# Attention with relative bias and an MLP on one core: where three pairs are turned, when one pair divides, and who copies out the last tiles

## The chip, the core and the metric

The kernel runs on one core of a Trainium2 chip. The metric is the time of one execution on the device in microseconds, as the median of several runs. A core has five engines that run their own instruction streams in order and wait for each other through semaphores: TensorE (PE, with weight loads shown apart as PEld), VectorE (DVE), ScalarE (ACT), GpSimd (POOL) and SyncE (SP). DMA transfers are issued from the streams of SP, POOL and ACT.

## The reference

Eight batches of eight heads, 576 positions, head size 64, float32. The bias depends only on the distance |i - j| through 32 buckets. Behind the attention comes an MLP with a leaky activation over 4608 tokens.

```python
scores = scale * np.matmul(q, k.transpose(0, 1, 3, 2))      # (8, 8, 576, 576)
bias = bias_table[bucket]                                     # bucket from |i - j|
scores = scores + bias.transpose(2, 0, 1)[None, :, :, :]
attn = np.exp(scores - np.max(scores, axis=-1, keepdims=True))
attn = attn / (np.sum(attn, axis=-1, keepdims=True) + 1e-09)
attn_out = np.matmul(attn, v)
x = attn_out.transpose(0, 2, 1, 3).reshape(B * S, H * D)      # (4608, 512)
h = x @ w_in                                                  # (4608, 2048)
g = np.maximum(0.01 * h, h)
out = g @ w_out                                               # (4608, 512) float32
```

## The kernel before

**Items.** The attention is worked off in 32 items, one for each batch and pair of heads, numbered from 0: item n is batch n // 4, heads 2(n % 4) and 2(n % 4) + 1. The "7th to 9th pair" of the change are items 6, 7 and 8; the 9th is the first of batch 2. For each item both heads' q and k must stand as (64 + 64) partitions by 576 positions (`qt`, `kt`); they arrive from memory as 96 rows by (head, 6 positions, 64), cast to bf16, in `qn` and `kn`.

**How q and k are turned.** There are two ways. For items 0 to 8, `turned_pair` (L267) makes twelve PE transposes for q and as many for k: each takes 96 rows of one head at one of six positions and writes 64 partitions of a PSUM bank from the pool `m`; DVE (q of early items: ACT) copies the bank to `qt` (L290) or `kt` (L294). From item 9 on (`by_dma`, L260), `pair_rows` (L252) first lays the two heads side by side in `pr` (two DVE copies of 96x768, L257), SP issues a transposing DMA from `pr` to `tu` (L265), and the same copies read `tu`.

**One body.** The loop over n (L867) runs item n's scores beside the second half of item n - 1. The order of the instructions on every engine is that of the program text. In a body: scores in PE (`qk_mm`, L312, L305 for the last 64 queries, L315 and L316 for the last 64 keys), exponentials on ACT (L325, L328, L332), the bias as a product with a band of exponentials on DVE (`band`, L348), the products with v (L361, L372 or, in halves of the rows, L407), the division on DVE (`divide`: a reciprocal L381 and a product L383 for each head, which empty the banks `o0` and `o1`), and the transposed result for the MLP (`x_transposes`: by DMA L423, or on PE L433 and a copy L434). The products L305 use `o0` and `o1` again, so they come behind the divisions. Between these stand pieces of the MLP: `ffn_in` (four products, L459, then the leaky step on ACT, L472, or on DVE, L467 and L470) and `ffn_out` (sixteen products in four parts, L486, then a copy to `y`, L504, and a store, L505). L459 and L486 take their banks from the pool `m` of two, like the transposes.

Bodies n = 5 and 6 have MLP input pieces alone (`room["only"]`): their last two pieces stand behind `band(n, 2)`, and L467 is the first DVE instruction of one of them. From n = 8 on most bodies run as `body_in_halves` (L629): there `av_phase` (L407) and pieces of the MLP (L610) run on the two halves of PE's rows, `fence` (L391) orders them, `transpose_q(n + 1)` stands ahead of `band(n, 0)` and `divide(n - 1, range(2))`, which divides both heads at once, and `score(n, 4)` (L305) follows behind the last L610 products. Body n = 8 is the first that copies q (of item 9) from a DMA's rows; that DMA is issued in body n = 7.

**Loads.** POOL issues all loads of q, k, v and the weights (L112 to L241), early items far ahead of their use; q and k of batch 2, first half of the heads, are issued in body n = 2.

**The end.** After the last item, `moe_rest` (L726) runs the rest of the MLP; its banks rotate over six. The last 128 products on PE are eight groups of sixteen L486: four of token tile 7, four of token tile 8. Seven groups are copied by DVE and stored by SP; the last group is copied and stored as two halves of 256 columns, one by DVE and SP, one by ACT and ACT's own queue (L491 to L498). Both halves read one PSUM bank, and the second copy waits for the first.

Of the kernel before, what the change touches and what calls it, by code (L numbers as in the profile page):

```python
# [37 lines left out]
def kernel(  # L38
# [10 lines left out]
    nc = tc.nc  # L49
# [217 lines left out]
    def turned_pair(n, j):  # L267

        if by_dma(n):
            return turned[n][:, j * NC : (j + 1) * NC, :].rearrange("p c r -> p r c")  # L270
        ps = ps_m_pool.tile([P, 8 * P], BF16, name="ps_t", tag="m")
        b, p = items[n]
        for c in range(NC):
            for e in range(2):
                nc.tensor.transpose(ps[e * D : (e + 1) * D, c * RQ : (c + 1) * RQ],
                                    in_=(qn, kn)[j][b % NBUF][0:RQ, 2 * p + e, c, :],
                                    identity=ident[0:RQ, 0:RQ])
        return ps[:, 0:S].rearrange("p (c r) -> p r c", c=NC)
# [55 lines left out]
    def band(n, u):  # L334
        b, p = items[n]
        at, at4 = at_view(n), at4_[n % 2]
        hp = hk[:, 2 * p : 2 * p + 2, :]
        if u == 0:
            o, m = at[:, :, 0, 0 : 2 * P], mirrored(hp, P, 3 * P)
        elif u in (1, 2):  # L340
            o, m = at[:, :, u, (u - 1) * P : (u + 2) * P], mirrored(hp, 0, 3 * P)
        elif u == NJ:
            o, m = at[:, :, 3, 2 * P : S], mirrored(hp, 0, S - 2 * P)
        elif u == NJ + 1:
            o, m = at4[:, 3 * P : S], mirrored(hk4[:, p, :], 0, P + SL)
        else:
            return
        nc.vector.tensor_tensor(out=o, in0=o, in1=m, op=ALU.mult)  # L348
# [27 lines left out]
    def divide(n, heads):  # L376
        opair = ops_[n]
        of = [outs[n][e][:, 0 : (NJ + 1) * (D + 1)].rearrange("p (i d) -> p i d", d=D + 1) for e in heads]
        rcps = [rc_pool.tile([P, NJ + 1, 1], FP32, name="rcp") for _ in heads]
        for ps, rcp in zip(of, rcps):  # L380
            nc.vector.reciprocal(rcp, ps[:, :, D : D + 1])  # L381
        for e, ps, rcp in zip(heads, of, rcps):
            nc.vector.tensor_tensor(out=opair[:, :, e * D : (e + 1) * D], in0=ps[:, :, 0:D],  # L383
                                    in1=rcp.to_broadcast([P, NJ + 1, D]), op=ALU.mult)
# [4 lines left out]
    def fence(sooner):  # L389

        f = nc.sync.nop(nofuse=True)  # L391
        tc.add_manual_dep(f.ins, sooner.ins.name, ended, reason="behind the last products of these rows")
        return f
# [83 lines left out]
    def ffn_out(T, s):  # L477

        t0 = T * TT
        gt, ts, part = gts[T], s // 4, s % 4  # L480
        if part == 0:
            outs_pm[T] = bank("pm2")
        pm = outs_pm[T]
        n = n_fc // 4
        for f in range(part * n, (part + 1) * n):
            nc.tensor.matmul(pm, lhsT=gt[:, f, ts * P : (ts + 1) * P], rhs=w_out_sb[:, f, :],  # L486
                             start=(f == 0), stop=(f == n_fc - 1))
        if part < 3:
            return
        o = out[t0 + ts * P : t0 + (ts + 1) * P, :]  # L490
        if T == n_tt - 1 and s == n_fc - 1:  # L491
            h = DM // 2
            for copy, queue, d in ((nc.vector.tensor_copy, nc.sync, slice(0, h)),
                                   (nc.scalar.copy, nc.scalar, slice(h, DM))):
                y = y_pool.tile([P, DM], FP32, name="y")
                copy(out=y[:, 0:h], in_=pm[:, d])
                queue.dma_start(out=o[:, d], in_=y[:, 0:h])
            return  # L498
        y = y_pool.tile([P, DM], FP32, name="y")
        if how["scalar"]:  # L500
            nc.scalar.copy(out=y, in_=pm)
            stores.append((o, y))
            return
        nc.vector.tensor_copy(out=y, in_=pm)  # L504
        nc.sync.dma_start(out=o, in_=y)  # L505
# [123 lines left out]
    def body_in_halves(n, kinds):  # L629

        loads(n)
        turns = rows_ahead(n) if by_dma(n + 1) else []
        score(n, 0)
        av_tails(n - 1)
        last = fence(av_phase(n - 1, 0))
        score(n, 1)
        T, s = made["out"], at_piece["out"]
        if kinds[0] == "out":
            one, two = open_piece("out", (T, s)), open_piece("out", (T, s + 4))
        else:  # L640
            one, two = open_piece("in"), open_piece("out")
        phase = side_by_side(one, two)
        phase(0, 0, 1)
        av_phase(n - 1, 1, last)
        if n + 1 < N:
            transpose_q(n + 1)
        band(n, 0)
        divide(n - 1, range(2))
        last = fence(phase(0, 1, n_cc))
        score(n, 2)  # L650
        score(n, 3)
        phase(1, 0, n_cc, last)
        band(n, 1)
        if n + 1 < N:
            transpose_k(n + 1)
        score(n, 4)
        if kinds[0] == "in":
            one[2]()
        late = [n - 1]
        if x_by_dma(n - 1):  # L660
            x_transposes(late.pop())
        for m in turns:
            turn_by_dma(m)
        while stores:
            o, y = stores.pop(0)
            nc.sync.dma_start(out=o, in_=y)
        band(n, 2)
        if kinds[0] == "out":
            outs_pm[T] = one[0]
            ffn_out(T, s + 1)  # L670
            band(n, 4)
            score(n, 5)
            band(n, 5)
            ffn_out(T, s + 2)
            ffn_out(T, s + 3)
            for m in late:
                x_transposes(m, "o0")
                finished(m)
            outs_pm[T] = two[0]
            for part in range(5, 8):  # L680
                ffn_out(T, s + part)
            at_piece["out"] = (s + 8) % n_fc
            made["out"] += at_piece["out"] == 0
            return
        piece_out()
        band(n, 4)
        score(n, 5)
        band(n, 5)
        piece_out()
        piece_out()  # L690
        for m in late:
            x_transposes(m, "o1")
            finished(m)
        room["left"] -= 5
        moe(room["left"], 0)
# [166 lines left out]
    moe(2)  # L862
    band(n, 5)
    band(n, 4)
    moe(1)

    for n in range(n_pairs + 1, N + 1):  # L867
# [43 lines left out]
            band(n, 1)  # L911
        band(n, 2)
        if room["only"]:
            exp(n, 3, ps_b)
            moe(2)
            exp(n, 4, ps_c)
            score(n, 5)
            T, f = step("in")
            room["left"] -= 1

            def last_bands():
                band(n, 5)
                band(n, 4)

            leaky(T, f, ffn_in(T, f), True, last_bands)
            moe(room["left"])
            continue
# [44 lines left out]
```

## Time and profile before

| | |
|---|---|
| Median of 3 runs | 375.03 us (374.81 to 375.28) |
| The profiled execution, its own time | 375.26 us |
| Its span, first to last instruction | 373.5 us |
| Granted clock of TensorE | 1.000 |
| Busy: PE, ACT, DVE, POOL | 357.6, 240.7, 196.5, 76.8 us |
| Items 9 on: DMA from `pr` to `tu` | 23 issues, 5.1 us from issue to landing (median) |
| Stores of 256 KB | 35, 2.4 us from issue to landing (median) |

How to read it: the chain of waits is followed back from the last instruction, at each step to what released it. A timeline row has the start in us, the length in us, the engine, the line, the operation and what it writes and reads; in brackets stands the idle time of the engine before it and what ended it. A row of the chain has start, length, engine, tile and line. In rows by group the length is the mean of one instruction in ns. PE's products overlap one another, so one lasts longer (379 ns for 512 columns) than the distance from one to the next.

### The profile page before, as it was taken

Reading aid. Unit: us, or ns where it says so; the run is one execution under the profiler, and the core shown is the slowest. Engines: PE = TensorE matmul, PEld = TensorE weight load, DVE = VectorE, ACT = ScalarE, POOL = GpSimd, SP = SyncE. Lnnn points to the kernel's source line nnn. Section 1 sums busy time; section 2 is a strip of 40 time slices with the busy share of each in tenths; the row PEclk is TensorE's granted clock in tenths of the full one; section 3 lists DMA queues with packets and bytes.
Section 4 is the critical chain, followed back from the end, with each engine's and each line's share of the span. In section 5 each row is a group of like instructions: output and inputs, shape, how many; then the busy total and the mean of one; then the engine's idle time right before and its main releaser. Section 6 shows DMA issues by size and latency. Waiting matters only on the chain.

```text
span 373.5 us, 10548 instructions
## 1 busy us (share of the span) xinstructions
PE 357.6 (96%) x4473; PEld 187.1 (50%) x4516; DVE 196.5 (53%) x504; ACT 240.7 (64%) x374; POOL 76.8 (21%) x118
## 2 busy tenths in 40 slices
PE   7889999999999999999999999999999999999994
PEld 2455555555455555555555555555555544444441
DVE  4688577776758566666755656665554200100121
ACT  5898886568856787777877777777777264064000
POOL 8763431333023303330233023100000000000000
PEclk9999999999999999999999999999999999999999
DMA  8999999999669979977798589833121000200221
GB/s 106 177 198 181 207 203 143 150 165 163 78 86 173 124 127 125 152 112 150 97 121 130 98 112 133 119 80 79 43 32 40 30 28 0 86 28 0 86 84 59
DMA packets 104360, 40.19 MB, mean 108 GB/s; under 512 B 83184, under 2 KB 98808, under 8 KB 104312
## 3 DMA queue, kind: packets, MB, share of 16 engines
q0 software_dynamic: 53696, 18.36, 47.6%
q1 hardware_dynamic: 50472, 21.02, 28.1%
q8 instruction: 35, 0.57, 0.6%
q10 hardware_dynamic: 144, 0.13, 0.1%
q14 instruction: 13, 0.11, 0.1%
HBM read 37.68 MB, written 9.45 MB: 126 GB/s over the span
## 4 chain that ended last, share of the span: by engine, by line
PE 87%; DVE 5%; ACT 4%; DMA 2%; issue 2%; DVEq 0%; ACTq 0%
PE pm L459 28%; PE pm L486 27%; PE pm L610 8%; PE ps_s L312 7%; PE ps_o L407 6%; PE ps_o L372 4%; ACT at L325 2%; DMA tu<-pr 2%; PE ps_s L315 2%; PE ps_o L361 1%; DVE opair L383 1%; PE ps_w L747 1%; DVE at L348 1%; PE ps_tx L433 1%; PE ps_q L305 1%
## 5 line engine op out<-in xcount | busy, mean ns | idle before, releaser
L325 ACT ACTIVATE at<-ps_s 128x1024 bf16<-128x1024 f32 x128 | 124.6, 1028 | 24.9 <-PE ps_s L312 24.8
L472 ACT ACTIVATE gt<-pm 128x512 bf16<-128x512 f32 x138 | 82.9, 605 | 71.1 <-PE pm L459 70.5
L459 PE MATMUL pm<-xT,w_in_sb 128*128 128x512 bf16 x490 | 117.2, 379 | 1.1
L486 PE MATMUL pm<-w_out_sb,gt 128*128 128x512 bf16 x468 | 109.3, 379 | 3.3 <-issue 3.0
L348 DVE TENSOR_TENSOR at<-at,hk 128x768 bf16<-128x768 bf16 (+3 forms) x160 | 71.0, 454 | 58.6 <-ACT at L325 34.2
L459 PEld LDWEIGHTS <-w_in_sb 128*128 128x128 bf16 x508 | 47.7, 98 | 54.7 <-issue 0.7
L486 PEld LDWEIGHTS <-gt 128*128 128x128 bf16 x492 | 45.0, 98 | 51.4
L504 DVE COPY y<-pm 128x512 f32<-128x512 f32 x35 | 24.2, 691 | 74.8 <-PE pm L486 72.1
L312 PE MATMUL ps_s<-qt,kt 64*128 64x512 bf16 x256 | 43.2, 380 | 3.6 <-ACT at L325 3.0
L610 PE MATMUL pm<-w_out_sb,gt 64*128 64x512 bf16 x168 | 42.0, 376 | 0.0
L610 PE MATMUL pm<-xT,w_in_sb 64*128 64x512 bf16 x136 | 37.5, 376 | 0.0
L119 POOL DMA_DIRECT2D vn<-in_v_dram x32 | 29.8, 939 | 11.1 <-PE pm L459 4.2
L383 DVE TENSOR_TENSOR opair<-ps_o,rcp 128x320 bf16<-128x320 f32 x64 | 29.7, 488 | 1.6
L769 POOL COPY tick<-opair 1x1 bf16<-1x1 bf16 x18 | 3.5, 194 | 130.5 <-DVE opair L383 130.5
L407 PE MATMUL ps_o<-vn,at 64*128 64x65 bf16 x1520 | 29.5, 190 | 0.0
L407 PEld LDWEIGHTS <-at 64*128 64x128 bf16 x1520 | 27.1, 94 | 4.3 <-SPq L391 3.0
L312 PEld LDWEIGHTS <-kt 64*128 64x128 bf16 x256 | 11.6, 94 | 25.5 <-issue 16.5
L332 ACT ACTIVATE at<-ps_s 128x576 bf16<-128x576 f32 x32 | 21.8, 683 | 0.7 <-PE ps_s L316 0.7
L381 DVE RECIPROCAL rcp<-ps_o 128x5 f32<-128x5 f32 x64 | 10.0, 181 | 22.3 <-PE ps_o L372 19.3
L328 ACT ACTIVATE at<-ps_q 128x256 bf16<-128x256 f32 x64 | 21.4, 396 | 0.5 <-PE ps_q L305 0.4
L372 PE MATMUL ps_o<-vn,at 128*128 128x65 bf16 x520 | 20.1, 194 | 0.0
L372 PEld LDWEIGHTS <-at 128*128 128x128 bf16 x520 | 17.9, 98 | 3.5 <-issue 0.7
(62 smaller groups left out, 243.3 us busy)
## 6 DMA issues: line engine op xcount, KB each, us to landing
out_dram<-y SPq DMA_DIRECT2D x35, 256.0 KB, 2.4
qn<-in_q_dram POOLq DMA_DIRECT2D x14, 288.0 KB, 6.3
kn<-in_k_dram POOLq DMA_DIRECT2D x14, 288.0 KB, 7.1
vn<-in_v_dram POOLq DMA_DIRECT2D x28, 128.0 KB, 5.9
w_in_sb<-in_moe_w_in_dram POOLq DMA_DIRECT2D x2, 1024.0 KB, 12.3
w_out_sb<-in_moe_w_out_dram POOLq DMA_DIRECT2D x2, 1024.0 KB, 15.8
qn<-in_q_dram POOLq DMA_DIRECT2D x4, 144.0 KB, 3.8
kn<-in_k_dram POOLq DMA_DIRECT2D x4, 144.0 KB, 4.0
```

What stands on the lines that cost most here:

```text
L119: nc.gpsimd.dma_start(out=vn[b % NBUF][:, c, h0:h1, 0:D], in_=v[b, h0:h1, c * P : (c + 1) * P, :].rearrange("h s d -> s h d"),)
L312: nc.tensor.matmul(ps[:, e, :], lhsT=kt[r, u * P : (u + 1) * P], rhs=qt[r, 0:512], start=True, stop=True)
L325: nc.scalar.activation(at[:, :, u, 0:512], ps, AF.Exp, scale=scale)
L348: nc.vector.tensor_tensor(out=o, in0=o, in1=m, op=ALU.mult)
L372: nc.tensor.matmul(ps[:, ic, :], lhsT=at[:, o : o + P], rhs=vn[b % NBUF][:, c, 2 * p + e, :], start=False, stop=(ic == NJ and c == NJ - 1))
L383: nc.vector.tensor_tensor(out=opair[:, :, e * D : (e + 1) * D], in0=ps[:, :, 0:D], in1=rcp.to_broadcast([P, NJ + 1, D]), op=ALU.mult)
L407: m = nc.tensor.matmul(outs[n][e][:, ic * (D + 1) : (ic + 1) * (D + 1)], lhsT=at[halves[r], o : o + P], rhs=vn[b % NBUF][halves[r], c, 2 * ...
L459: nc.tensor.matmul(pm, lhsT=w_in_sb[:, c, f * P : (f + 1) * P], rhs=xT[c][:, t0 : t0 + TT], start=(c == 0), stop=(c == n_cc - 1))
L472: nc.scalar.activation(g, pm, AF.Prelu, bias=0.0, scale=1.0, alpha=0.01)
L486: nc.tensor.matmul(pm, lhsT=gt[:, f, ts * P : (ts + 1) * P], rhs=w_out_sb[:, f, :], start=(f == 0), stop=(f == n_fc - 1))
L504: nc.vector.tensor_copy(out=y, in_=pm)
L610: m = nc.tensor.matmul(pm, lhsT=w[halves[r]], rhs=x[halves[r]], start=(k == 0 and c == 0), stop=(low is not None and k == 1 and c == n_cc ...
```

## The change

It has three parts.

1. `pair_rows` is also called for items 6, 7 and 8: for item 6 at the end of body n = 4 (behind `band(4, 4)`), for items 7 and 8 in bodies n = 5 and 6 behind `band(n, 2)`, ahead of the last MLP pieces. `turned_pair` then makes six PE transposes of 96 rows by 128 columns (both heads) instead of twelve of 96 by 64. On DVE that adds three times two copies of 96x768; on PE 36 transposes with their weight loads fall away, and 36 of the double width stay where 72 stood.
2. In body n = 8, `transpose_q(9)` moves behind `band(8, 0)` and `divide(7, ...)`. On DVE the copy L290 thus follows the two L381 and two L383 instead of standing ahead of the band.
3. Once all input pieces of the MLP are made, output tiles are copied by ACT and stored from ACT's queue instead of by DVE and SP: seven tiles of 128x512. The last group's parts 0 to 2 do nothing; with part 3 it runs sixteen products of 384 columns in one bank and then sixteen of 128 columns in another, each part copied by ACT and stored from ACT's queue behind its last product.

No other instruction changes its place on any engine.

```diff
@@ turned_pair
         for c in range(NC):
+            if n > n_pairs + 1:
+                nc.tensor.transpose(ps[:, c * RQ : (c + 1) * RQ], in_=prs[n][:, j, c, :],
+                                    identity=ident[0:RQ, 0:RQ])
+                continue
             for e in range(2):
@@ ffn_out
         n = n_fc // 4
+        o = out[t0 + ts * P : t0 + (ts + 1) * P, :]
+        if T == n_tt - 1 and ts == 3:
+            if part < 3:
+                return
+            for d in (slice(0, 3 * P), slice(3 * P, DM)):
+                w = d.stop - d.start
+                pm = bank("pm2")
+                for f in range(n_fc):
+                    nc.tensor.matmul(pm[:, 0:w], lhsT=gt[:, f, ts * P : (ts + 1) * P], rhs=w_out_sb[:, f, d],
+                                     start=(f == 0), stop=(f == n_fc - 1))
+                y = y_pool.tile([P, DM], FP32, name="y")
+                nc.scalar.copy(out=y[:, 0:w], in_=pm[:, 0:w])
+                nc.scalar.dma_start(out=o[:, d], in_=y[:, 0:w])
+            return
         for f in range(part * n, (part + 1) * n):
...
-        o = out[t0 + ts * P : t0 + (ts + 1) * P, :]
-        if T == n_tt - 1 and s == n_fc - 1:
-            h = DM // 2
-            for copy, queue, d in ((nc.vector.tensor_copy, nc.sync, slice(0, h)),
-                                   (nc.scalar.copy, nc.scalar, slice(h, DM))):
-                y = y_pool.tile([P, DM], FP32, name="y")
-                copy(out=y[:, 0:h], in_=pm[:, d])
-                queue.dma_start(out=o[:, d], in_=y[:, 0:h])
-            return
         y = y_pool.tile([P, DM], FP32, name="y")
         if how["scalar"]:
             nc.scalar.copy(out=y, in_=pm)
             stores.append((o, y))
+            return
+        if made["in"] == n_tt:
+            nc.scalar.copy(out=y, in_=pm)
+            nc.scalar.dma_start(out=o, in_=y)
             return
         nc.vector.tensor_copy(out=y, in_=pm)
         nc.sync.dma_start(out=o, in_=y)
@@ body_in_halves
         av_phase(n - 1, 1, last)
-        if n + 1 < N:
+        late_q = n == 2 * n_pairs
+        if n + 1 < N and not late_q:
             transpose_q(n + 1)
         band(n, 0)
         divide(n - 1, range(2))
+        if late_q:
+            transpose_q(n + 1)
         last = fence(phase(0, 1, n_cc))
@@ body n = n_pairs
     band(n, 5)
     band(n, 4)
+    pair_rows(n + 2)
     moe(1)
@@ loop over n
         band(n, 2)
         if room["only"]:
+            if not by_dma(n + 2):
+                pair_rows(n + 2)
             exp(n, 3, ps_b)
             moe(2)
```

## The prediction, made before the changed kernel ran

> **What bounds it now.** I read the page first, then the chain of waits merged in order of time, then the timeline of the places where that chain leaves TensorE.
>
> ```profile
> span 373.5 us, 10548 instructions
> PE 357.6 (96%) x4473; PEld 187.1 (50%) x4516; DVE 196.5 (53%) x504; ACT 240.7 (64%) x374; POOL 76.8 (21%) x118
> PE 87%; DVE 5%; ACT 4%; DMA 2%; issue 2%; DVEq 0%; ACTq 0%
> ```
>
> TensorE (PE) carries 87% of the chain. So work taken from PE, or a gap of PE closed, shortens the run; work added to VectorE (DVE) or ScalarE (ACT) costs only where PE ends up waiting for it. The one large piece of the chain off PE is a DMA, around the body n = 8 (items count from 0: the 7th to 9th pairs are items 6 to 8):
>
> ```profile
> 59.68 7.71 DMA tu<-pr
> 67.42 0.65 DVE qt L290
> ...
> 69.99 0.81 PE pm L486 x3
> ```
>
> It does not hold PE for 7.7 us; the timeline of that place shows what it does cost:
>
> ```profile
> 66.44 0.78 PE L407 MATMUL ps_o<-vn,at 64*128 64x65 bf16 x40
> 66.54 0.35 DVE L257 COPY pr<-kn 96x768 bf16<-96x768 bf16 x1
> 67.42 0.65 DVE L290 COPY qt<-tu 128x576 bf16<-128x576 bf16 x1 [0.53 <-DMA tu<-pr]
> 67.99 0.42 DVE L348 TENSOR_TENSOR at<-at,hk 128x512 bf16<-128x512 bf16 x1
> 68.13 1.03 PE L610 MATMUL pm<-w_out_sb,gt 64*128 64x512 bf16 x8
> 68.32 0.26 DVE L381 RECIPROCAL rcp<-ps_o 128x5 f32<-128x5 f32 x2
> 68.61 0.89 DVE L383 TENSOR_TENSOR opair<-ps_o,rcp 128x320 bf16<-128x320 f32 x2
> 69.56 0.27 PE L305 MATMUL ps_q<-qt,kt 64*128 64x64 bf16 x7 [0.19 <-DVE opair L383]
> ```
>
> DVE stands 0.53 us until item 9's transposed rows land, then copies q (0.65); only then do the band and the two divisions (L381, L383) follow. PE's products of L305 write the banks that the divisions read, so PE waits for L383.
>
> **Part 1, the divisions ahead of q's copy (n = 8).** The next body shows the same place without the wait:
>
> ```profile
> 78.69 0.38 PE L610 MATMUL pm<-xT,w_in_sb 64*128 64x512 bf16 x1
> 79.55 0.28 PE L305 MATMUL ps_q<-qt,kt 64*128 64x64 bf16 x8
> 79.99 0.38 PE L486 MATMUL pm<-w_out_sb,gt 128*128 128x512 bf16 x1 [0.16 <-issue]
> 69.89 0.65 DVE L294 COPY kt<-tu 128x576 bf16<-128x576 bf16 x1
> 75.57 0.39 PE L312 MATMUL ps_s<-qt,kt 64*128 64x512 bf16 x2
> ```
>
> The first three rows are n = 9. From the start of its eight L610 products (the first row is one of them) it is 0.86 to L305 and 1.30 to L486. For n = 8 that would be 68.13 + 0.86 = 68.99 and 68.13 + 1.30 = 69.43; L486 started at 69.99 (the chain above): the stall is 0.56 us. In the changed order DVE is free at 66.54 + 0.35 = 66.89, does the band (0.42) to 67.3, starts the reciprocals when L407 has ended (66.44 + 0.78 = 67.22), and has divided by 67.3 + 0.26 + 0.89 = about 68.55, 0.4 ahead of 68.99. The stall goes whole: -0.56. What moves behind is q's copy, to 68.55 to 69.2: it no longer waits (the rows landed at 67.40), k's copy of item 9 (69.89, fourth row) stays within 0.1 us, and the scores that use both start at 75.57. Its cover is those 6 us; without it, it would cost its 0.65. Bounds: 0 and -0.56.
>
> **Part 2, whole pairs transposed on PE.** Six sets (q and k of items 6, 7, 8) of twelve 96x64 transposes become six of 96x128. Rows for the size:
>
> ```profile
> 48.56 0.38 PE ps_t L275 x12
> 56.54 0.72 PE ps_o L372 x20
> 72.77 0.28 PE ps_tx L433 x5
> L372 PEld LDWEIGHTS <-at 128*128 128x128 bf16 x520 | 17.9, 98 | 3.5 <-issue 0.7
> ```
>
> A set takes 0.38 now. A 128x128 transpose costs 0.28/5 = 56 ns. The 512-column products pass a column in 0.42 ns (Part 3), so 128 columns are 54 of the 56, and 96 columns are 40; with 3 over, 43 ns, so 0.26 a set: -0.12. Ends: 63 ns (a pair of halves as now, 0.38/6; no gain) and 40 ns (-0.14). For q the whole 0.12 reaches the path in all three bodies, as PE goes straight on to L459, the second head and its reciprocal: -0.36 (0 to -0.42). For k in n = 5 and 6 something else ends last:
>
> ```profile
> 42.09 0.49 DVE L383 TENSOR_TENSOR opair<-ps_o,rcp 128x320 bf16<-128x320 f32 x1
> 42.50 0.75 DVE L294 COPY kt<-ps_t 128x576 bf16<-128x576 bf16 x1
> 43.30 1.89 PE L459 MATMUL pm<-xT,w_in_sb 128*128 128x512 bf16 x7
> ```
>
> L459 needs the bank that k's copy empties at 43.25, and that copy starts behind a division, not behind the transposes; 0 there (to -0.28). In n = 7 PE has no such wait: -0.12 (0 to -0.14).
>
> DVE pays with three times two copies of 96x768, about 0.35 each (the L257 row above), in gaps it has:
>
> ```profile
> 39.90 0.20 DVE L381 RECIPROCAL rcp<-ps_o 128x5 f32<-128x5 f32 x1 [2.83 <-PE ps_o L372]
> 46.33 0.69 DVE L467 TENSOR_SCALAR low<-pm 128x512 bf16<-128x512 f32 x1 [1.52 <-PE pm L459]
> 55.02 0.69 DVE L467 TENSOR_SCALAR low<-pm 128x512 bf16<-128x512 f32 x1 [1.53 <-PE pm L459]
> 35.20 0.67 POOL L112 DMA_DIRECT2D kn<-in_k_dram  x1 [0.24 <-DMA vn<-in_v_dram]
> kn<-in_k_dram POOLq DMA_DIRECT2D x1, 288.0 KB, 14.8
> ```
>
> The copies stand just ahead of these three instructions, 0.70 into gaps of 2.83, 1.52 and 1.53: nothing, and 0.70 each if the gap were gone, because L467, the last bands and L470 queue behind them. Item 8's rows are the latest to arrive, at 35.20 + 14.8 = 50.0, against a read at 55.02 - 1.53 = 53.5.
>
> **Part 3, the last rows.** Now:
>
> ```profile
> 340.60 27.51 PEld L486 LDWEIGHTS <-gt 128*128 128x128 bf16 x128
> 368.64 0.42 DVE L496 COPY y<-pm 128x256 f32<-128x256 f32 x1 [2.76 <-PE pm L486]
> 369.10 0.37 ACT L496 COPY y<-pm 128x256 f32<-128x256 f32 x1 [27.49 <-DVE y L496]
> 369.50 0.37 ACTq L497 DMA_DIRECT2D out_dram<-y  x1
> L472 ACT ACTIVATE gt<-pm 128x512 bf16<-128x512 f32 x138 | 82.9, 605 | 71.1 <-PE pm L459 70.5
> out_dram<-y SPq DMA_DIRECT2D x7, 256.0 KB, 2.0
> out_dram<-y SPq DMA_DIRECT2D x1, 128.0 KB, 1.7
> out_dram<-y ACTq DMA_DIRECT2D x1, 128.0 KB, 2.5
> q14 instruction: 3, 0.02, 1.5%
> ```
>
> The two half copies run one behind the other: DVE's starts 0.02 after PE's end (368.62), ACT's ends at 369.47: 0.85. Afterwards the last group is 16 products of 384 columns, then 16 of 128. The 128 weight loads start 27.4/127 = 216 ns apart, one 512-column product each, so 384 take 162 and 128 take 56 (the L433 row): 3.49 against 3.45, +0.04. The 384 part is copied and issued while PE makes the 128 part (0.9 us): the copy takes about 0.49 and the issue 0.37, just in time. ACT from 256 to 512 columns goes from 372 to 605 ns, 0.91 a column, so the 128-column copy takes 256: 0.28 after PE's end, -0.57. Seven full copies also go from DVE to ACT (about 0.6 every 3.45 us; ACT did nothing there) and their stores from SP's queue to ACT's: nothing, as PE alone sets that stretch, and a full copy and issue would have to outlast 3.45 us to cost. Landing: the last store now takes 2.5, though SP's equal half took 1.7 and a store of twice the size 2.0; in that stretch instruction fetches (q14) run on the same engines. I take 2.0 for the 64 KB, between 1.7 and 2.5, since the fetch may meet it again: -0.5 (0 to -0.8).
>
> The Trainium skill, page "DMA: Bandwidth & Descriptors", section "Anatomy of one DMA", fits 2.0 us + bytes/436e9 for GpSimd's path; by it (an estimate) 64 KB land in 2.15, 0.35 sooner than now instead of 0.5; SP's 1.7 lies under its fixed part.
>
> **Sum**: -0.56 - 0.36 - 0.12 + 0.04 - 0.57 - 0.5 = -2.07. Against the profiled execution's own 375.26: 373.2. That execution lies 0.23 above the median of the runs, so the median goes from 375.03 to **373.0**.
>
> **Rivals.**
> - The 64-wide halves already pass side by side, and a whole one takes as long as two. For: twelve in 0.38 are 32 ns each, less than the 40 that 96 columns need. Against: the L433 row. Part 2 brings 0: 373.5.
> - PE's gain in the middle (1.04) is given back at a later wait: some operand that comes by DMA is met 1 us sooner. For: DMA is busy there. Against: item 9's is the only such wait in the list. Only the tail stays, -1.03: 374.0.
> - As before, and the last store again lands in 2.5: -0.53, 374.5, not told from no change (0.2%, 0.75 us, is about what can be).
> - Slower: a stationary operand of 128 columns whose load is not hidden. 36 transposes and 16 narrow products would each cost its 98 ns (L372 row): 36 x 0.098 - 6 x 0.38 = +1.25, tail 16 x (0.098 + 0.162) - 3.45 = +0.71, less 0.56 and 0.57, landing 2.5: +0.83, 375.9. It decides from 82 ns a product on. Against: L372's twenty with 128x128 weights take 0.72, 36 ns each.
>
> The Trainium skill, page "TensorE: Matmul & The Clock Gate", section "Part 3: Packing small matmuls", says that a weight load overlaps running products only where its row group differs; all these use the same rows, so it speaks for that last rival. The trace disagrees: 36 ns a pair against loads of 98.
>
> **How the numbers follow.** Forecast 0.50; halves side by side 0.18; only the tail 0.17; as before 0.10; slower 0.05. Faster by over 0.2% (under 374.28): 0.50 + 0.18 + 0.17 = 0.85; within 0.10; slower 0.05. The largest gain of all bounds is 0.56 + 0.42 + 0.28 + 0.14 + 0.53 + 0.8 = 2.73, 372.3; the upper end takes in the tail-only case: 372.2 to 374.3.
>
> **What would show it.** Right: a set of six transposes in about 0.26; no idle time of DVE at q's copy of item 9 and L486 1.3 behind the eight L610's start; from the last product to the last issue about 0.3; the last store landing near 2.0. Wrong: a set still at 0.38; L305 still waiting for L383; an idle PE behind L467 or the pair copies; a landing of 2.5; a gap that opens behind n = 9.

## The result and the profile after

| | before | after |
|---|---|---|
| Median | 375.03 us (374.81 to 375.28) | 372.27 us (372.04 to 372.53, 4 runs) |
| Ratio, with its 95% interval | | 0.9921 (0.9908 to 0.9933) |
| The profiled execution, its own time | 375.26 us | 372.35 us |
| Its span | 373.5 us | 370.6 us |

The kernel became faster by 2.8 us in the medians, 2.9 in the two profiled executions. The forecast was 373.0, 0.7 above the measured median; the median stands at the low end of the range (372.2), and the ratio times 375.03, 372.07, lies 0.1 below it. The longest runs had a lower granted clock: the five longest of the kernel before among the experiments (377.1 us and over) had a mean clock of 0.991 to 0.996, and the longest run without part 1 there, 379.64 us at 0.991, is left out of its ratio.

Lines of the changed kernel are shifted: L376 is L372 of before, L463 is L459, L504 is L486, L623 is L610, L387 is L383, L316 is L312, L309 is L305, L471 is L467, and q's copy L294 is L290. L275 is now the whole-pair transpose and L279 the one in halves.

The page of the changed kernel, the busy times and the chain by engine:

```profile
span 370.6 us, 10507 instructions
PE 356.3 (96%) x4453; PEld 187.7 (51%) x4496; DVE 192.9 (52%) x502; ACT 245.4 (66%) x382; POOL 76.4 (21%) x118
PE 87%; ACT 4%; DMA 3%; DVE 3%; issue 2%; POOL 0%; ACTq 0%; DVEq 0%; POOLq 0%
```

PE's busy time fell by 1.3 us only, and its share of the chain is still 87%: the rest of the 2.9 us are idle stretches, so they have to be looked for place by place.

**The transposed sets.** PE's timeline of before, first the surroundings of q's set in n = 5, then the first of the four score products at four points (start, length, engine, line, what it writes and reads, count):

```profile
38.39 0.61 PE L312 MATMUL ps_s<-qt,kt 64*128 64x512 bf16 x4
...
39.08 0.78 PE L372 MATMUL ps_o<-vn,at 128*128 128x65 bf16 x20
39.79 0.45 PE L275 MATMUL ps_t<-ident,qn 96*64 96x96 bf16 x12
40.17 1.04 PE L459 MATMUL pm<-xT,w_in_sb 128*128 128x512 bf16 x3
...
47.09 0.61 PE L312 MATMUL ps_s<-qt,kt 64*128 64x512 bf16 x4
...
55.78 0.61 PE L312 MATMUL ps_s<-qt,kt 64*128 64x512 bf16 x4
...
60.48 0.61 PE L312 MATMUL ps_s<-qt,kt 64*128 64x512 bf16 x4
```

The same view of the changed kernel:

```profile
38.14 0.60 PE L316 MATMUL ps_s<-qt,kt 64*128 64x512 bf16 x4
...
38.83 0.78 PE L376 MATMUL ps_o<-vn,at 128*128 128x65 bf16 x20
39.45 0.42 PE L275 MATMUL ps_t<-ident,pr 96*128 96x96 bf16 x6
39.71 1.03 PE L463 MATMUL pm<-xT,w_in_sb 128*128 128x512 bf16 x3
...
46.61 0.61 PE L316 MATMUL ps_s<-qt,kt 64*128 64x512 bf16 x4
...
55.08 0.61 PE L316 MATMUL ps_s<-qt,kt 64*128 64x512 bf16 x4
...
59.33 0.61 PE L316 MATMUL ps_s<-qt,kt 64*128 64x512 bf16 x4
```

From score to score it was 8.70, 8.69 and 4.70 us; it is 8.47, 8.47 and 4.25. That is -0.23 for n = 5, -0.22 for n = 6 and -0.45 for n = 7 (the last stretch holds both of its sets): -0.90, where the prediction had -0.48. The six whole transposes pass in 39.71 - 39.45 = 0.26 instead of 0.38, as forecast. But by the starts the row ahead of them became shorter too: the set now begins 0.62 behind the start of the twenty products, 0.71 before. That second piece, 0.09 a set, was not in the sum. The chain of waits, which goes by ends, has it on the row behind the set instead; this is that row in the chain of before and in that of the changed kernel, n = 5:

```profile
40.24 0.32 PE pm L459
```

```profile
39.87 0.22 PE pm L463
```

The first row also shows something that the change does not touch: the changed kernel was already 0.25 ahead at 38 us, where both programs had run the same transposes. That is scatter from execution to execution: in two further executions of the changed kernel (below) the same point lies at 38.82 and 38.58.

**DVE's cover.** DVE's timeline, the instruction behind the two pair copies in n = 5 and in n = 6:

```profile
45.86 0.69 DVE L471 TENSOR_SCALAR low<-pm 128x512 bf16<-128x512 f32 x1 [0.98 <-PE pm L463]
...
54.32 0.69 DVE L471 TENSOR_SCALAR low<-pm 128x512 bf16<-128x512 f32 x1 [0.99 <-PE pm L463]
```

DVE still waits 0.98 and 0.99 us for PE there (1.52 and 1.53 before), so the copies, which take 0.54 of each gap, delay nobody.

**Body n = 8.** The changed kernel's timeline, DVE and PE:

```profile
66.45 0.89 DVE L387 TENSOR_TENSOR opair<-ps_o,rcp 128x320 bf16<-128x320 f32 x2
66.99 1.03 PE L623 MATMUL pm<-w_out_sb,gt 64*128 64x512 bf16 x8
67.85 0.28 PE L309 MATMUL ps_q<-qt,kt 64*128 64x64 bf16 x8
68.18 0.76 DVE L294 COPY qt<-tu 128x576 bf16<-128x576 bf16 x1 [0.84 <-DMA tu<-pr]
68.29 0.81 PE L504 MATMUL pm<-w_out_sb,gt 128*128 128x512 bf16 x3 [0.16 <-issue]
```

L623 to L309 is 0.86 and to L504 1.30, the distances of a body without the stall. DVE waited for item 9's rows even longer than before (0.84, not 0.53), but now the divisions stand ahead of that wait, and PE lost nothing. The lead over before grew from 1.15 us at the last score row above to 69.99 - 68.29 = 1.70 at L504: 0.55, forecast 0.56.

**Body n = 25.** The chain, and PE's timeline at its end:

```profile
214.65 9.21 DMA xT<-opair
```

```profile
223.13 0.37 PE L623 MATMUL pm<-xT,w_in_sb 64*128 64x512 bf16 x1
...
223.90 0.37 PE L623 MATMUL pm<-xT,w_in_sb 64*128 64x512 bf16 x1 [0.39 <-DMA xT<-opair]
```

Two products that otherwise start 0.22 apart started 0.77 apart, since the transposed rows of item 23 landed 9.2 us after their issue. 0.55 us of the lead went here, in this one execution: in the two further profiled executions of the same kernel (below) PE does not wait at this place.

**The end.** The timeline of PE and ACT, and the last two stores (queue, operation, count, size, us to landing):

```profile
363.85 3.66 PE L497 MATMUL pm<-w_out_sb,gt 128*128 128x384 bf16 x32
...
367.60 0.27 ACT L500 COPY y<-pm 128x128 f32<-128x128 f32 x1 [0.47 <-PE pm L497]
367.89 0.34 ACTq L501 DMA_DIRECT2D out_dram<-y  x1
```

```profile
out_dram<-y ACTq DMA_DIRECT2D x1, 192.0 KB, 1.9
out_dram<-y ACTq DMA_DIRECT2D x1, 64.0 KB, 1.6
```

PE ends at 363.85 + 3.66 = 367.51. The last copy ends at 367.87, 0.36 later (0.85 before); the store is issued at 367.89 and lands in 1.6 (2.5 before), at 369.49; the span ends 1.1 later (373.5 - 369.50 - 2.5 = 1.5 before). From PE's end to the end of the span it is 3.09 us, 4.88 before: -1.79, forecast -1.07.

The whole account of the profiled pair: start -0.25, sets -0.90, n = 8 -0.55, n = 25 +0.55, narrow products and rounding +0.04, end -1.79: -2.90. The first and the fourth are not the change's own.

### The profile page after: what moved, and what is told of

Read it like the earlier page. It is cut to its first block, busy times and chain, and to the rows that moved or that the text cites. A ratio compares the mean times of both kernels' runs of the same rounds, so it can differ in the third digit from the quotient of the medians.

```text
span 370.6 us, 10507 instructions
## 1 busy us (share of the span) xinstructions
PE 356.3 (96%) x4453; PEld 187.7 (51%) x4496; DVE 192.9 (52%) x502; ACT 245.4 (66%) x382; POOL 76.4 (21%) x118
## 4 chain that ended last, share of the span: by engine, by line
PE 87%; ACT 4%; DMA 3%; DVE 3%; issue 2%; POOL 0%; ACTq 0%; DVEq 0%; POOLq 0%
PE pm L463 28%; PE pm L504 27%; PE pm L623 8%; PE ps_s L316 8%; PE ps_o L411 6%; PE ps_o L376 4%; DMA xT<-opair 2%; ACT at L329 2%; PE ps_s L319 2%; PE ps_o L365 1%; DVE opair L387 1%; PE ps_tx L437 1%; PE ps_q L309 1%; DMA kn<-in_k_dram 1%; PE pm L497 1%
## 5 line engine op out<-in xcount | busy, mean ns | idle before, releaser
L463 PE MATMUL pm<-xT,w_in_sb 128*128 128x512 bf16 x490 | 117.2, 379 | 1.1
L504 PE MATMUL pm<-w_out_sb,gt 128*128 128x512 bf16 x452 | 105.9, 379 | 3.3 <-issue 3.0
L463 PEld LDWEIGHTS <-w_in_sb 128*128 128x128 bf16 x508 | 47.8, 98 | 54.5 <-issue 0.7
L504 PEld LDWEIGHTS <-gt 128*128 128x128 bf16 x476 | 43.5, 98 | 49.5
L316 PE MATMUL ps_s<-qt,kt 64*128 64x512 bf16 x256 | 43.3, 380 | 3.6 <-ACT at L329 3.0
L623 PE MATMUL pm<-w_out_sb,gt 64*128 64x512 bf16 x168 | 42.2, 376 | 0.0
L517 DVE COPY y<-pm 128x512 f32<-128x512 f32 x28 | 19.4, 691 | 40.9 <-PE pm L504 38.1
L623 PE MATMUL pm<-xT,w_in_sb 64*128 64x512 bf16 x136 | 37.7, 376 | 0.4 <-DMA xT<-opair 0.4
L387 DVE TENSOR_TENSOR opair<-ps_o,rcp 128x320 bf16<-128x320 f32 x64 | 29.7, 488 | 1.6
L316 PEld LDWEIGHTS <-kt 64*128 64x128 bf16 x256 | 11.6, 94 | 25.4 <-issue 16.5
L376 PE MATMUL ps_o<-vn,at 128*128 128x65 bf16 x520 | 20.1, 194 | 0.0
L376 PEld LDWEIGHTS <-at 128*128 128x128 bf16 x520 | 17.9, 98 | 3.5 <-issue 0.7
```

Source lines behind the costliest of these rows:

```text
L316: nc.tensor.matmul(ps[:, e, :], lhsT=kt[r, u * P : (u + 1) * P], rhs=qt[r, 0:512], start=True, stop=True)
L376: nc.tensor.matmul(ps[:, ic, :], lhsT=at[:, o : o + P], rhs=vn[b % NBUF][:, c, 2 * p + e, :], start=False, stop=(ic == NJ and c == NJ - 1))
L463: nc.tensor.matmul(pm, lhsT=w_in_sb[:, c, f * P : (f + 1) * P], rhs=xT[c][:, t0 : t0 + TT], start=(c == 0), stop=(c == n_cc - 1))
L623: m = nc.tensor.matmul(pm, lhsT=w[halves[r]], rhs=x[halves[r]], start=(k == 0 and c == 0), stop=(low is not None and k == 1 and c == n_cc ...
```

## The experiments

The kernel before, run again beside these kernels on three chips, scattered more than in the first runs: medians 375.56, 375.56 and 375.45 (57 runs, 374.55 to 378.1). Each ratio below is against the runs of before on the same chip; a kernel with one run has no interval.

| kernel | median us (lowest to highest, runs) | ratio (95%) |
|---|---|---|
| part 1 alone | 375.79 (374.54 to 377.43, 12) | 1.0008 (0.9990 to 1.0027) |
| part 2 alone | 374.34 (373.35 to 375.76, 12) | 0.9963 (0.9947 to 0.9980) |
| part 3 alone | 373.48 (373.00 to 373.99, 6) | 0.9944 (0.9926 to 0.9962) |
| the change again | 372.40 (372.21 to 372.52, 4) | 0.9913 (0.9893 to 0.9932) |
| the change a third time | 372.36 (372.21 to 374.82, 6) | 0.9921 (0.9897 to 0.9945) |
| without part 1 | 374.04 (372.84 to 379.64, 7) | 0.9952 (0.9932 to 0.9972) |
| without the seven full tiles on ACT | 373.66 (373.14 to 375.25, 11) | 0.9944 (0.9925 to 0.9963) |
| before, 8 more DVE instructions | 374.57 (374.17 to 377.36, 11) | 0.9974 (0.9954 to 0.9994) |
| items 4 and 5 whole too | 373.54 (373.02 to 374.08, 6) | 0.9942 (0.9924 to 0.9960) |
| halves out of `pr` | 373.17 (1) | |
| only the k sets whole | 373.28 (1) | |
| one position of six in halves | 374.04 (1) | |

### Each part alone, and all of them again

Each is the kernel before with one part of the diff shown above; the fourth kernel is the changed one.

```diff
@@ part 1 alone: body_in_halves
-        if n + 1 < N:
+        late_q = n == 2 * n_pairs
+        if n + 1 < N and not late_q:
             transpose_q(n + 1)
...
+        if late_q:
+            transpose_q(n + 1)
@@ part 2 alone: turned_pair, and the two calls of pair_rows
+            if n > n_pairs + 1:
...
+    pair_rows(n + 2)
...
+            if not by_dma(n + 2):
+                pair_rows(n + 2)
@@ part 3 alone: ffn_out
+        if T == n_tt - 1 and ts == 3:
...
+        if made["in"] == n_tt:
```

> Only the divisions ahead of q's copy in body n = 8; all else as before. My account: DVE's wait for item 9's rows goes and PE's wait for the divisions with it, 0.56 us between bodies 8 and 9 and nowhere else, so 374.5 if the gain lasts to the end. Rival: the gain is given back at a later DMA operand (in the changed kernel 0.57 us went again in body n = 25, where PE waited for xT); then 375.0.

> Only the transposes of whole pairs for items 6 to 8; all else as before. My account now: a set saves 0.22 us, 0.12 in the transposes themselves and 0.10 in the step from the 128x65 products to them; both sets of bodies 7 and the q sets of bodies 5 and 6 reach the path: 0.88 us by body 8, 374.15. As recorded: 0.12 a set, 0.48 in all, 374.55. Item 9's rows are then the later ones at body 8, so DVE's wait there should grow and may take back part of the 0.88.

> Only the change at the end (copies and stores by ACT, last rows in two parts); all else as before. My account: the end comes 0.56 us earlier by the copies, 0.9 by the landing, 0.4 by SP's last waits, less 0.05 to 0.1 for the narrow products: 1.8 us, 373.2. As recorded: 1.03, 374.0, with the last store landing in 2.0.

> The changed kernel once more. If the wait for xT in body n = 25 belongs to the new times, it is there again and the runs lie at 372.3. If it came from one late transfer, it is gone or elsewhere in this profile, and the span is nearer 370.0.

Against before on the same chip the parts bring +0.23, -1.22 and -2.08, together -3.07; all of them together -3.16. That the two agree is luck: each interval is 1.2 to 1.5 us wide, part 1's gain is not in its median, and part 2 alone also ends 0.7 sooner, because its last store lands in 1.8 us and not in 2.5, a gain that part 3 brings as well.

The profiles add up better. From the first scores of n = 5 to PE's end it is 330.21 us before (38.39 to 368.60), 329.64 with part 1 alone, 329.37 with part 2 alone, and 328.80 with all parts, in two executions (329.37 in the first one, with its wait in n = 25). So part 1 gives 0.57 there, part 2 0.84 and both together 1.41. From PE's end to the end of the span it is 4.9 before and with part 1 alone, and 3.1 with part 3 alone and with all of them.

Part 2 alone shows the scores at 39.42, 47.90, 56.36 and 60.61 us: stretches of 8.48, 8.46 and 4.25, a gain of 0.90 again, of which 0.05 goes to a longer stall in n = 8 (0.61, with a wait of 0.60 for item 9's rows). Part 3 alone has the same end as the changed kernel: its last store is issued at 368.54, lands in 1.6, and the span ends at 371.2, 1.1 after that. In part 1 alone PE's timeline has the eight L610 products at 68.65 and L486 at 69.95, the 1.30 of a body without the stall, and by the sums above the gain lasts to PE's end. In the time of that execution (375.27) it isn't seen, since it came to the first scores of n = 5 at 38.92, 0.53 later than before. That point lies anywhere from 38.14 to 39.46 in the fourteen profiles, also for one and the same kernel; what sets it is open. It is open too why the median of the twelve runs shows no gain: their interval (0.9990 to 1.0027) leaves out one of 0.56 us (0.9985). The counter-experiment (without part 1) is below.

In the second execution of the whole change PE doesn't wait in n = 25, nor in the third. So that wait is not a property of the change; none of the other thirteen profiles has it. The span did not come near 370.0 all the same: it was 370.7, as the first scores of n = 5 came 0.68 later than in the first execution.

### Part 2: what a set of halves costs

The recorded term was 0.12 a set, the traces show 0.22. Three kernels look for the rest: the halves taken out of `pr` (is it the source?), the k sets alone whole (which sets reach the path?), one of the six positions left in two halves (is it the halves, or the switch between them and whole products?).

```diff
@@ halves out of pr
             if n > n_pairs + 1:
-                nc.tensor.transpose(ps[:, c * RQ : (c + 1) * RQ], in_=prs[n][:, j, c, :],
-                                    identity=ident[0:RQ, 0:RQ])
+                for e in range(2):
+                    nc.tensor.transpose(ps[e * D : (e + 1) * D, c * RQ : (c + 1) * RQ],
+                                        in_=prs[n][:, j, c, e * D : (e + 1) * D],
+                                        identity=ident[0:RQ, 0:RQ])
@@ only the k sets whole
-            if n > n_pairs + 1:
+            if n > n_pairs + 1 and j == 1:
@@ one position of six in halves
-            if n > n_pairs + 1:
+            if n > n_pairs + 1 and c != NC // 2:
```

> The changed kernel, but the rows in pr are again turned in twelve 96x64 transposes a set: the source, DVE's copies and all else stay. Before, the halves started in pairs every 43 ns, the rate of the whole ones now; what a set of halves costs more would then be the two steps into it and out of it, about 0.09 us each. So: from the first L376 to the first L463 behind q's set 1.09 us again (0.88 in the changed kernel), bodies 5, 6 and 7 longer by 0.22, 0.22 and 0.44. Rival: the source made the difference (qn and kn against pr); then bodies as in the changed kernel.

> The changed kernel, but only k's sets are whole pairs; q's are twelve halves. If k's gain in bodies 5 and 6 is hidden behind DVE's copy of k, as recorded, these two bodies are as long as before the change (8.70 from scores to scores) and body 7 alone is 0.22 shorter than before. Rival: k's sets gain 0.22 in each of the three.

> The changed kernel, but of the six positions of each set the fourth is turned as two halves, the other five whole. If the two steps between whole and half operands cost 0.09 us each, a set loses nearly all its gain: bodies 5, 6 and 7 are longer by 0.2, 0.2 and 0.4 than in the changed kernel. If each half product were the dearer one, a sixth of 0.22 is lost: 0.04, 0.04 and 0.07.

Halves out of `pr`, PE's timeline, the last two score rows (L318 is L316 there):

```profile
56.02 0.61 PE L318 MATMUL ps_s<-qt,kt 64*128 64x512 bf16 x4
...
60.72 0.60 PE L318 MATMUL ps_s<-qt,kt 64*128 64x512 bf16 x4
```

4.70, the distance of before: where the rows come from makes no difference. With only the k sets whole:

```profile
47.67 0.61 PE L316 MATMUL ps_s<-qt,kt 64*128 64x512 bf16 x4
...
56.36 0.61 PE L316 MATMUL ps_s<-qt,kt 64*128 64x512 bf16 x4
...
60.83 0.60 PE L316 MATMUL ps_s<-qt,kt 64*128 64x512 bf16 x4
```

n = 5 takes 8.70 (from 38.97) and n = 6 8.69 as before, so k's set brings nothing there, and n = 7 takes 4.47 instead of 4.70, so it brings 0.23. That is the prediction's split of the sets: three for q and one for k, 4 x 0.22 = 0.88. With one position in halves, PE's timeline of q's set in n = 5:

```profile
40.15 0.78 PE L376 MATMUL ps_o<-vn,at 128*128 128x65 bf16 x20
40.77 0.29 PE L275 MATMUL ps_t<-ident,pr 96*128 96x96 bf16 x3
40.99 0.23 PE L279 MATMUL ps_t<-ident,qn 96*64 96x96 bf16 x2
41.16 0.26 PE L275 MATMUL ps_t<-ident,pr 96*128 96x96 bf16 x2
41.26 1.03 PE L463 MATMUL pm<-xT,w_in_sb 128*128 128x512 bf16 x3
```

This set holds five whole products and one pair of halves, and from L376 to L463 it takes 1.11, no less than the 1.09 of before with six pairs. At 43 ns a product the first three should last 0.13, but it is 0.22 to the halves; the pair should last 0.04, but it is 0.17 to the next whole one. The last two go at the usual pace (0.10). So the halves themselves cost no more than whole products, a pair of them in 43 ns; going from products that use the whole width of PE to such that use half, and back, costs 0.09 + 0.13 = 0.22 us, and once a set, with one pair of halves between as with six. The three bodies take 8.71, 8.69 and 4.70 in this kernel, as before the change. In the trace's single records of before, the load of the first half of this set starts 0.15 us behind the load ahead of it, and that of the first L459 0.18 behind the last half's, where loads, or pairs of them, otherwise follow each other at 0.03 to 0.04: at both switches the next load starts late. Why it does is not shown.

### The end: landing, pauses and the seven tiles

Before, the last store (128 KB) landed in 2.5 us, its equal on SP's queue in 1.7. Two suspects: the instruction fetches (q14), which share the DMA engines, and ACT's queue itself. Eight more instructions on DVE ahead of `moe_rest` move the rest of DVE's stream and leave the code of the end as it is:

```diff
@@ moe_rest of the kernel before
+        for _ in range(8):
+            nc.vector.memset(warm, 0.0)
```

> The kernel before with eight memsets of one column on DVE ahead of the last MLP part, where DVE has nothing to do. If the last store of before landed late (2.5 us) because an instruction fetch, set off by the count of DVE's instructions, met it on one DMA engine, the fetch now comes earlier: landing 1.75, the end about 0.5 to 0.7 us earlier than before with the same copies. Rival: ACT's queue is slower at its first store; then 2.5 again and no change.

The last stores of this kernel in the view of its DMA:

```profile
out_dram<-y SPq DMA_DIRECT2D x1, 128.0 KB, 1.7
out_dram<-y ACTq DMA_DIRECT2D x1, 128.0 KB, 1.7
```

The same store on the same queue lands in 1.7 now. The view of the DMA, taken over the time in which this store's packets move, has two instruction fetches in before (369.5 to 371.5 us) and in part 1 alone (369.46 to 371.51), where the landing is 2.5 as well. It has none in this kernel up to 372.6 (one begins at 372.63, beside the last packets), and none in part 2 alone (369.69 to 371.1), which has six more DVE instructions and the end of before, and lands in 1.8. So the queue is not the cause: the store lands late where two fetches fall among its packets. That they are fetches of DVE's instructions, and meet it on the same DMA engine, is inferred; no row names either. The last 1.5 us, from landing to the end of the span, stay as they were. In the medians this kernel is 0.99 us faster than before, more than the 0.7 of its end; its profiled execution, 376.32, is one of its longest, because of a long stall in n = 8 (below).

For the other two pieces of the end, the seven full tiles went back to DVE and SP, and only the last group kept its new form:

```diff
@@ ffn_out of the changed kernel
-        if made["in"] == n_tt:
-            nc.scalar.copy(out=y, in_=pm)
-            nc.scalar.dma_start(out=o, in_=y)
-            return
```

> The changed kernel, but the seven full tiles at the end are copied by DVE and stored by SP as before; only the last group is ACT's. Copies and landing as in the changed kernel (0.29 and 1.6). If SP's 0.37 us pause among its last waits belongs to SP's own instruction count, it is back with SP's seven stores and the end is 0.4 later than in the changed kernel: 372.8. Rival: the pause went with the order of the last stores; then 372.4.

Its timeline of the end:

```profile
364.23 3.66 PE L497 MATMUL pm<-w_out_sb,gt 128*128 128x384 bf16 x32
...
367.54 0.37 ACTq L501 DMA_DIRECT2D out_dram<-y  x1
368.46 0.27 ACT L500 COPY y<-pm 128x128 f32<-128x128 f32 x1 [0.95 <-PE pm L497]
368.75 0.34 ACTq L501 DMA_DIRECT2D out_dram<-y  x1
```

PE ends at 367.89, and the last copy starts at 368.46, 0.57 later instead of 0.09, although ACT had been through with the issue at 367.91. The view by line shows the semaphore waits at L500, here (from 366 us on) and in the changed kernel (from 364 us on; the first of its two stands ahead of the first copy):

```profile
L500 ACTq EVENT_SEMAPHORE  x3: 38/38/38, 368.2 to 368.4; - x3
```

```profile
L500 ACTq EVENT_SEMAPHORE  x2: 17/17/17, 365.0 to 367.5; - x2
```

So ACT has three waits ahead of this copy and not one. But the first of the three starts only 0.32 us after the issue (0.04 in the changed kernel), and they follow each other at 0.08: of the 0.48 that the copy is later, about 0.28 is this pause and 0.2 are the waits. In before, a pause of the same 0.32 stands at the same place of ACT's stream, behind its 575th record of the trace; there it falls behind the last issue and holds up no copy. The store lands in 1.6 again, at 370.35, and the span ends at 371.9: 1.55 later, 1.1 in the changed kernel. So without the seven tiles the end is longer by 0.48 + 0.45 = 0.93, of the 1.3 us that the medians differ by (on different chips; 0.9 to 1.2 by the ratios). Only the 0.4 was expected. PE itself is not touched: from the first scores of n = 5 to its end it is 328.80, as in the changed kernel.

The 1.5 us stand in all five kernels that have the seven stores on SP's queue (before, part 1 alone, part 2 alone, 8 more instructions, this one), the 1.1 in the nine that don't. The trace's records of SP's last waits show why: in each of the five a pause of 0.34 to 0.36 us stands behind SP's 207th record, after the landing of the last store (372.14 to 372.49 in before). The nine have 198 records on SP and no such pause. So it is SP's own stream that ends later, and the order of the last stores, which is the new one here, is not the reason. What the two pauses are stays open.

### Part 1 taken away

```diff
-        late_q = n == 2 * n_pairs
+        late_q = False
```

> The changed kernel with q's copy of item 9 ahead of the band and the divisions again. Bodies 5 to 7 now end 0.9 us sooner while item 9's rows land about as late as before, so DVE waits longer for them and PE for DVE: at least 0.56 us more between bodies 8 and 9, 372.9 to 373.5, and more where the transfer is late in a run. Rival: part 1 is worth nothing in the time, as the comparison of part 1 alone read (375.79 against 375.56); then 372.4.

Its timeline of n = 8:

```profile
67.06 1.03 PE L623 MATMUL pm<-w_out_sb,gt 64*128 64x512 bf16 x8
67.15 0.65 DVE L294 COPY qt<-tu 128x576 bf16<-128x576 bf16 x1 [1.34 <-DMA tu<-pr]
68.35 0.89 DVE L387 TENSOR_TENSOR opair<-ps_o,rcp 128x320 bf16<-128x320 f32 x2
68.89 0.20 PE L309 MATMUL ps_q<-qt,kt 64*128 64x64 bf16 x1 [0.81 <-DVE opair L387]
69.72 0.81 PE L504 MATMUL pm<-w_out_sb,gt 128*128 128x512 bf16 x3 [0.16 <-issue]
```

L623 to L504 takes 2.66 instead of 1.30: the stall is 1.36 here, 0.56 in the profile of before, because the rows were waited for 1.34 instead of 0.53. In the profile of the kernel with eight more DVE instructions (DVE's timeline) the wait is longer still:

```profile
69.20 0.65 DVE L290 COPY qt<-tu 128x576 bf16<-128x576 bf16 x1 [2.00 <-DMA tu<-pr]
```

There the stall is 2.03, which is why that execution was long. Part 3 alone has a wait of 0.31 and a stall of 0.33. So with the old order the stall follows the landing of item 9's rows, which differs from execution to execution, and the divisions ahead of the wait take it out whole, whatever its length (0.84 us of waiting in the changed kernel cost nothing). Beside the other two parts, part 1 is worth 374.04 - 372.36 = 1.68 in the medians, 1.2 by the ratios (0.9952 against 0.9921, of 375; the intervals overlap), and 1.36 in the profile, more than the 0.56 of the prediction each time.

### Further whole pairs, and the change a third time

If a set gives 0.22, items 4 and 5 might give it too.

```diff
@@ turned_pair
-            if n > n_pairs + 1:
+            if n > n_pairs - 1:
@@ the first bodies, behind band(n, 2)
+        if n > 1:
+            pair_rows(n + 2)
```

> The changed kernel with whole pairs for items 4 and 5 too, their rows set in bodies 2 and 3 behind band 2. Bodies 3 and 4: body 3 is paced by ACT's exponentials (one every us), so nothing there; in body 4 q's set of item 5 saves up to 0.2 us, k's is behind the division. 372.2 to 372.4. Against it: two more copies on DVE in bodies 2 and 3, where it has little idle time; if they hold up the bands, slower by up to 1.4.

> The changed kernel beside the other three: 372.4. In its profile the last store lands in 1.6, no pause among SP's last waits, and bodies 5, 6 and 7 at 8.47, 8.47 and 4.25 to the second scores. A wait for xT in body 25 only if one transfer is late.

With items 4 and 5 too, the kernel is slower than the changed one by 1.2 us in the medians and by 0.8 in the profiled pair (spans 371.2 and 370.4). Its list of waits between 24 and 40 us (engine and line that waited, for whom, us in total, times, longest) and DVE's timeline:

```profile
PE ps_t L275 <- DVE pr L257: 1.1, 1, 1.1
```

```profile
24.92 0.72 DVE L257 COPY pr<-kn 96x768 bf16<-96x768 bf16 x1
```

PE waits 1.1 us for the pair copies there, one of which took 0.72 instead of 0.35. Not all of it is lost, as PE waits 0.7 for ACT in that stretch of the changed kernel; but 0.4 for a band, behind the other two copies, comes on top. Where DVE has no gap ahead of the transposes, the cover that part 2 relies on is missing, and the copies cost more than whole transposes bring. The third run of the change (span 370.4) again has no wait in n = 25. None of the kernels tried beats the changed one.

## Why the prediction was too small, and what of it held

The forecast was faster by 2.07 us. By the profiles, the change itself is worth 3.2: 1.41 from the first scores of n = 5 to PE's end, where the sum had 1.00, and 1.8 behind it, where the sum had 1.07. The direction and the places of the gain were right. Three terms failed: part 2's 0.12 a set (0.42 short over the sets), the landing of 2.0 us (0.4 short), and the "nothing" for the seven full copies (0.4 short). That the first profiled pair shows 2.9, nearer to the forecast, is luck: 0.55 went at one late DMA in n = 25, and 0.25 came from the start.

- **Part 1, "the stall goes whole: -0.56".** Right: 0.55, with 1.30 between the two rows that were named for it. That q's copy "no longer waits" was wrong: it waited 0.84, and k's copy came 0.6 later after the eight L610, not within 0.1, but the scores that use both come later still, so it cost nothing. The size is that of one execution: with the old order the wait was 0.31, 0.53, 0.60, 1.34 and 2.00 us in five profiles, and the stall with it. The prediction took one landing for the usual one. (Its 67.3 + 0.26 + 0.89 is 68.45, not 68.55; nothing hangs on it.)
- **Part 2, "-0.12 a set".** The mis-sized term on PE. "A set takes 0.38 now" went to 0.26 as forecast, but not because halves pass at 63 ns a pair: they pass at 43, and the 0.12 is the way back to whole-width products behind the last of them. The way there, 0.09, is not in the set's own row: by the starts it stands on the row ahead (0.71 to the set's start, 0.62 where whole transposes follow), in the chain of waits on the row behind (0.32, and now 0.22). It was left out, so 0.12 a set should have been 0.22. The end "-0.14" fell with it, and with that the range's low end, which summed such ends (and was given as 372.2 where its sum is 372.3).
- **Part 2, k's sets "0 there" for n = 5 and 6, one set for n = 7.** Right, by the kernel with only the k sets whole. The copies' cover was right too: gaps of 0.98 and 0.99 remain, and where there is none (items 4 and 5) the loss is 0.8 to 1.2.
- **Rival "the halves already pass side by side".** Its premise is right: a pair of halves takes 43 ns like a whole one. Its conclusion, 0 for part 2, is wrong, since it left out the two switches as well.
- **Part 3, products and copies.** "+0.04" and "-0.57": the account leaves +0.04 for the products, and the copies gave 0.49, since the last one starts 0.09 after PE's end rather than with it.
- **Part 3, landing "2.0".** 1.6 in every kernel with the new last group: -0.9 instead of -0.5. The fetch, kept in the estimate with half its price, did not meet the store there. The Trainium skill, page "DMA: Bandwidth & Descriptors", section "Anatomy of one DMA", would give 2.15 for 64 KB by its fit for GpSimd's path (an estimate); on ACT's queue the runs stay below even its fixed part of 2.0.
- **Part 3, the seven full copies: "nothing".** Wrong. The stretch itself is PE's, as said, but the last instructions of two streams are not: SP ends 0.4 sooner behind the last landing, and without these copies ACT would have lost 0.5 ahead of its last one, to a pause and two more waits. The sum held neither.
- **Rival "given back at a DMA wait".** It came true once (0.55 in n = 25 of the first profiled execution), not in two others.
- **Rival "slower", weight loads that aren't hidden.** Excluded: six whole transposes with their loads pass in 0.26. The Trainium skill, page "TensorE: Matmul & The Clock Gate", section "Part 3: Packing small matmuls", lets a load overlap running products only where its row group differs; the trace disagrees with that rule, at 43 ns a transpose whose own load (96x128) lasts 97 ns. It agrees with the other way that the same section names, a load into a background weight buffer.

What stays open: why part 1 alone isn't seen in the median of its runs, though its profile has 0.57 up to PE's end and taking it away costs 1.2 to 1.7; what moves the first scores of n = 5 by up to 1.3 us between executions; and what the pauses in SP's and ACT's streams are.

## What to carry to other kernels

Price a group of instructions from the start of the one ahead to the start of the one behind; a chain of waits books the cost of a switch on its neighbours. Put the work that others wait for ahead of an instruction that waits for a DMA, even if the profile shows a short wait there: it is the mean of the landings that counts, and one execution shows one of them. Compare stretches between two named rows rather than whole spans: here the start alone moved by 1.3 us. At the end of a kernel every engine's last instructions and waits can be on the path, also those of engines that did nothing that mattered before.

## What was not expected of the hardware

- Between products that use PE's whole width (128 columns) and such that use half of it, each way costs about 0.1 us (0.09 in, 0.13 out), while pairs of halves among themselves go at 43 ns like whole ones.
- The landing of the last store changed from 2.5 to 1.7 us with eight instructions more on an engine that has no part in it; with 2.5, two instruction fetches fell among its packets, with 1.7 none did until the last of them.
- An idle ACT began a copy 0.57 us after the product that it needed, with a pause of 0.32 and three waits of 0.08 each in its stream ahead of it, and 0.09 after it with one wait and no pause.
- SP's stream has a pause of 0.34 to 0.36 us at one and the same place, behind its 207th record, in each of five kernels that get that far; with the last waits beyond that place, the span ends 0.4 later.
